# Joining the two words of a double with an integer addition on the weights' conversion

## The chip, the cores and the metric

One core of a Trainium2 chip runs the kernel. The metric is the device time of one execution in microseconds (us). The core has a matrix engine (TensorE, PE in the rows; PEld is its weight load), VectorE (DVE), ScalarE (ACT), GpSimd (POOL) and SyncE (SP), which issues the DMA transfers here. Each engine works through its own instructions in the order in which they stand and waits where an operand isn't ready.

## The reference

An attention with 32 inducing points is followed by two feed-forward layers. With x of 12480 x 128, inducing of 32 x 128 and four weight matrices of 262144 elements each:

```
def mab(q, kv):
    s = scale * (q @ kv.transpose(0, 2, 1)); s = s - s.max(-1, keepdims=True)
    a = np.exp(s); a /= a.sum(-1, keepdims=True) + 1e-09
    return a @ kv
h = mab(I, x)                      # 32 x 128
x = mab(x, h)                      # 12480 x 128
h = x @ w_in;   x = np.maximum(0.01 * h, h) @ w_out            # 2048 wide
h = x @ w2_in;  g = where(h >= 1, h, where(h <= -1, 0, (h + 1) ** 2 / 4));  x = g @ w2_out
```

The weights arrive as doubles (the drawn values are multiplied to float64), that is, as two 32-bit words per element, low word first.

## The kernel before

**Stages.** First the x tokens are read in nine bands and the inducing points attend to them (lines 330 to 378); that gives HT. Then 25 chunks of some 500 tokens each pass through the rest. The loop from line 604 runs over column steps k: chunk c and block j of 128 hidden columns, k = 16 c + j. In one step PE makes block j of the hidden layer of chunk c (line 626, from Gs, which is HT times the first weights, and the attention weights aT). ACT rounds it to hi (line 629). DVE makes the rest lo (line 636), or at j = 4, 8, 12 of chunk 0 and 3, 9, 14 of the next chunks ACT makes r and POOL subtracts (lines 633, 634). D1 = 4 steps later PE multiplies hi and lo with the second weights, whi[0] and wlo[0], in three matmuls (L577 in all rows of PE, since a helper records them). The second layer (weights n = 2, 3) starts 86 steps later and runs beside the first until the end.

**Weights.** The four matrices are cut into 16 units (n, q), n the matrix and q a quarter of 512 columns. A unit's words come by one DMA of 512 KB into a tile wraw (10 buffers, column 2i the low word and 2i + 1 the high word of element i). The generator convert(n, q) turns them into fp32 for n = 0 (tile w1) and into a rounded part whi and a rest wlo for n = 1 to 3. Its buffers cva and cvb exist three times. Two units run at a time; each call of work(1) takes one of them, in turns, to its next yield. Line 339 to 347, 586 to 600 and 710 to 713 call it: in the bands as WORK_S says, four times around the first attention of a chunk, once in each of the steps k = 0 to 15 and once in three steps after that. So the place of a conversion's instruction in an engine's order follows from how many yields lie ahead of it. The order of the units is (0,0), (1,0), (0,1), (0,2), (1,1), (0,3), (1,2), (1,3), then n = 2 and n = 3.

**One unit before.** ACT takes the high word times 2^-112 without its sign (L108), DVE the sign bit (L109), DVE joins them by shift and or (L111): cva is the high word's value as fp32. DVE cuts out its power of two (L113) and multiplies the low word by 2^-52 and by this power (L118): cvb is the low word's value. For n = 0 DVE adds both (L121). For n > 0 ACT rounds cva to whi (L116), and POOL takes cva minus whi (L125) plus cvb (L126) for wlo; for (1,0) and (1,1) PE does that instead with three matmuls by unit matrices (L134, L135, L136) and ACT reads the result (L137).

**What waits for it.** hidden(q, .) multiplies HT with a quarter of w1 into Gs (PE L403, ACT L407, DVE L410); linear(.) folds the slope of the first layer into Qs (L425 to L445), and the loop reads whi and wlo of a matrix from the step on where ensure() stands.

Of the kernel before, what the change touches and what calls it, by code (L numbers as in the profile page):

```python
# [9 lines left out]
F32 = mybir.dt.float32  # L10
F32R = mybir.dt.float32r
I32 = mybir.dt.int32
U32 = mybir.dt.uint32
AF = mybir.ActivationFunctionType
ALU = mybir.AluOpType
# [18 lines left out]
QW = 512  # L34
# [31 lines left out]
PE_LO = 2  # L66
# [6 lines left out]
def moe_kernel(ctx: ExitStack, tc, x_d, xf_d, xl_d, xt_d, it_d, w1_d, w2_d, w3_d, w4_d, y_d):  # L73


    nc = tc.nc
# [7 lines left out]
    cv = fill.enter_context(tc.tile_pool(name="cv", bufs=3, side="right"))  # L84
    xp = fill.enter_context(tc.tile_pool(name="xp", bufs=1, side="right"))
    ps = ctx.enter_context(tc.tile_pool(name="ps", bufs=1, space=PSUM))
    bank = [ps.tile([128, 512], F32, name=f"bank{i}", tag=f"bank{i}") for i in range(8)]
# [10 lines left out]
    def convert(n, q):  # L98

        t = raws.pop((n, q))
        up, low = t[:, :, 1], t[:, :, 0]
        sl = slice(q * QW, (q + 1) * QW)
        a = cv.tile([128, QW], F32, name="cva")
        b = cv.tile([128, QW], F32, name="cvb")
        au, bu = a.bitcast(U32), b.bitcast(U32)
        nc.scalar.activation(a, up.bitcast(F32), AF.Abs, scale=WORD_SCALE)  # L108
        nc.vector.tensor_scalar(out=bu, in0=up.bitcast(U32), scalar1=0x80000000, scalar2=None, op0=ALU.bitwise_and)  # L109
        yield  # L110
        nc.vector.scalar_tensor_tensor(out=au, in0=au, scalar=3, in1=bu, op0=ALU.logical_shift_left, op1=ALU.bitwise_or)  # L111
        yield
        nc.vector.tensor_scalar(out=bu, in0=au, scalar1=0xFF800000, scalar2=None, op0=ALU.bitwise_and)  # L113
        if n:
            hi, lo = whi[n - 1][:, sl], wlo[n - 1][:, sl]
            nc.scalar.activation(hi, a, AF.Copy)  # L116
        yield
        nc.vector.scalar_tensor_tensor(out=b, in0=low.bitcast(U32), scalar=2.0 ** -52, in1=b, op0=ALU.mult, op1=ALU.mult)  # L118
        if n == 0:
            yield  # L120
            nc.vector.tensor_tensor(out=w1[:, sl], in0=a, in1=b, op=ALU.add)  # L121
        elif n == 1 and q < PE_LO:
            lows.append((bank[2 + q], a, b, hi, lo))
        else:
            nc.gpsimd.tensor_tensor(out=a, in0=a, in1=hi.bitcast(F32), op=ALU.subtract)  # L125
            nc.gpsimd.tensor_tensor(out=lo, in0=a, in1=b, op=ALU.add)  # L126

    lows = []

    def low_parts(n):  # L130

        for _ in range(n):
            s, a, b, hi, lo = lows.pop(0)
            nc.tensor.matmul(s, lhsT=ident, rhs=a, start=True, stop=False)  # L134
            nc.tensor.matmul(s, lhsT=ident, rhs=b, start=False, stop=False)  # L135
            nc.tensor.matmul(s, lhsT=nidentr, rhs=hi, start=False, stop=True)  # L136
            nc.scalar.activation(lo, s, AF.Copy)  # L137

# [8 lines left out]
    def work(n, until=len(units)):  # L147

        for _ in range(n):
            while len(running) < 2 and to_convert and len(units) - len(to_convert) < until:  # L150
                running.append((to_convert[0], convert(*to_convert.pop(0))))
            if not running:
                return
            u, r = running.pop(0)
            if next(r, "end") != "end":
                running.append((u, r))
            else:
                done.add(u)
                if ahead:
                    load_next_w()  # L160

    def ensure(n, j):

        while (n, j * 128 // QW) not in done:
            work(1)
        if n == 1:
            low_parts(len(lows))
# [17 lines left out]
    w1 = fillp.tile([128, FF], F32, name="w1")  # L185
    whi, wlo = [wts.tile([128, FF], F32R, name="whi0", tag="whi0")], [wts.tile([128, FF], F32R, name="wlo0", tag="wlo0")]
# [32 lines left out]
    ident = const.tile([128, 128], F32, name="ident")  # L219
# [110 lines left out]
    for s in range(NS_B):  # L330
        ready = len(lows)
        scores(s)
        if s:
            turn(s - 1)
        warm(WARM_A.get(s, 0))
        if s + 1 < NS_B and s + 1 not in xT:
            by_channel(s + 1)
        exps(s)
        work(WORK_S[s][0], UNTIL_S[s])
        if s:  # L340
            gather(s - 1)
            add_up(s - 1)
        if s >= NS_B - XL:
            warm(WARM_B)
        if s == NS_B - 3:
            low_parts(ready)
        work(WORK_S[s][1], UNTIL_S[s])
# [29 lines left out]
                            in1=rden[:, None, :].to_broadcast([C, 3, M]), op=ALU.mult)  # L377
# [226 lines left out]
    for k in range(NS + LAG * NJ + OB + D2):  # L604
# [18 lines left out]
        if in_a:  # L623
# [3 lines left out]
            hi = hp1.tile([128, CW], F32R, name="hi1")[:, :w]  # L627
            lo = hp1.tile([128, CW], F32R, name="lo1")[:, :w]
            nc.scalar.activation(hi, p1, AF.Relu)  # L629
            h1[k] = hi, lo  # L630
            if j in (POOL_LO1 if kb >= 0 else POOL_LO1_FILL if c else POOL_LO1_0):
                r = r1p.tile([128, CW], F32, name="r1")[:, :w]
                nc.scalar.activation(r, p1, AF.Relu)  # L633
                nc.gpsimd.tensor_tensor(out=lo, in0=r, in1=hi.bitcast(F32), op=ALU.subtract)  # L634
            else:
                nc.vector.scalar_tensor_tensor(out=lo, in0=p1, scalar=0.0, in1=hi.bitcast(F32),  # L636
                                               op0=ALU.max, op1=ALU.subtract)
# [6 lines left out]
        if kb - 2 in gs:  # L644
            g = gs.pop(kb - 2)
            hi = hp3.tile([128, CW], F32R, name="hi3")[:, :g.shape[1]]
            lo = hp3.tile([128, CW], F32R, name="lo3")[:, :g.shape[1]]
# [15 lines left out]
        if kb - 1 in sqs:  # L663
# [4 lines left out]
                                           op0=ALU.max, op1=ALU.add)  # L668
            gs[kb - 1] = g
        if late:  # L670
            lo, g, hi = late
            nc.vector.tensor_tensor(out=lo, in0=g, in1=hi.bitcast(F32), op=ALU.subtract)
        if 0 <= kh < NS:
# [5 lines left out]
            if jh == NJ - 1:  # L679
                mm(px, Qs, aT.pop(ch), False, True)  # L680
                hi = x2p.tile([128, CW], F32R, name="x2hi")[:, :w]
                lo = x2p.tile([128, CW], F32R, name="x2lo")[:, :w]
# [18 lines left out]
        if k in HIDDEN:  # L701
            q = 1 + HIDDEN.index(k)
# [3 lines left out]
        if k == HIDDEN[-1]:  # L706
            low_parts(len(lows))
# [58 lines left out]
```

## Time and profile before

| | us |
|---|---|
| median of 3 runs | 1000.36 (999.27 to 1000.88) |
| the profiled execution | 1000.86 |
| its span in the trace | 998.9 |
| PE busy in the span | 980.3 |
| DVE busy | 812.6 |
| ACT busy | 798.7 |
| POOL busy | 642.9 |

The span runs from the first to the last instruction that the profiler recorded; some 2 us of the execution lie outside. The granted clock of TensorE was 0.999 of full speed over the span. Rows name instructions by the line of the kernel, the operation and the tiles (out<-in); a wait stands in brackets as the idle time ahead of an instruction and what released it.

### The profile page before, as it was taken

What the parts mean: (1) busy time and instruction counts of PE and PEld (TensorE: products, weight loads), DVE (VectorE), ACT (ScalarE), POOL (GpSimd) and SP (SyncE); (2) the same over time, 40 slices, a digit from 0 to 9 for tenths busy, and PEclk for the clock granted to TensorE, in tenths of its full rate; (3) what the DMA queues carried; (4) which work ended last, traced back from release to release, by engine and by line L of the source; (5) the groups of instructions that cost most, each with busy time, mean ns of one, the idle gap of its engine ahead of it and who ended that gap; (6) DMA issues with size and microseconds to landing.
All of it is one profiled execution on the core that took longest, in us unless ns stands there. A gap on an engine that the chain in (4) does not pass through costs nothing.

```text
span 998.9 us, 14767 instructions
## 1 busy us (share of the span) xinstructions
PE 980.3 (98%) x4632; PEld 797.0 (80%) x4632; DVE 812.6 (81%) x1358; ACT 798.7 (80%) x1464; POOL 642.9 (64%) x513
## 2 busy tenths in 40 slices
PE   8889999999999999999999999999999999999998
PEld 6656777888878888878888878888888888888886
DVE  4799888877779877779877779777788777789997
ACT  4576778888878888878888878888878888889997
POOL 0044546667766666666766666666667667778886
PEclk9999999999999999999999999999999999999999
DMA  9801011100002000001000001000000000000000
GB/s 351 322 28 38 1 58 43 42 1 11 11 1 68 27 1 12 11 27 52 17 1 12 11 22 41 11 1 11 12 1 27 11 1 12 11 12 11 12 10 22
DMA packets 18863, 34.22 MB, mean 34 GB/s; under 512 B 10928, under 2 KB 14128, under 8 KB 17504
## 3 DMA queue, kind: packets, MB, share of 16 engines
q1 hardware_dynamic: 18784, 33.28, 9.6%
q8 instruction: 36, 0.59, 0.2%
q14 instruction: 43, 0.35, 0.1%
HBM read 22.66 MB, written 6.39 MB: 29 GB/s over the span
## 4 chain that ended last, share of the span: by engine, by line
PE 92%; DVE 5%; ACT 1%; issue 1%; POOL 1%; ACTq 0%; POOLq 0%; DVEq 0%
PE bank L577 87%; DVE lo L636 2%; PE bank L263 1%; PE bank L275 1%; PE bank L308 1%; DVE cva L111 1%; PE bank L474 1%; PE bank L233 0%; PE bank L326 0%; ACT hi L629 0%; PE bank L297 0%; POOL lo L634 0%; DVE cvb L113 0%; POOL wlo L126 0%; DVE cvb L118 0%
## 5 line engine op out<-in xcount | busy, mean ns | idle before, releaser
L653 POOL TENSOR_TENSOR lo<-g,hi 128x500 fp32r<-128x500 f32 (+2 forms) x392 | 496.5, 1270 | 205.8 <-PE bank L577 150.1
L629 ACT ACTIVATE hi<-bank 128x500 fp32r<-128x500 f32 (+2 forms) x400 | 233.9, 588 | 133.2 <-PE bank L577 128.8
L577 PE MATMUL bank<-lo,whi 128*128 128x500 f32 (+2 forms) x800 | 311.5, 389 | 3.2 <-POOL lo L634 2.8
L577 PE MATMUL bank<-hi,whi 128*128 128x500 f32 (+2 forms) x800 | 311.1, 389 | 0.0
L577 PE MATMUL bank<-hi,wlo 128*128 128x500 f32 (+2 forms) x800 | 310.4, 388 | 0.0
L661 DVE TENSOR_SCALAR cl<-bank 128x500 f32<-128x500 f32 (+2 forms) x400 | 268.0, 670 | 43.6 <-PE bank L577 37.5
L641 ACT ACTIVATE sq<-cl,half 128x500 f32<-128x500 f32 (+2 forms) x400 | 284.3, 711 | 17.7 <-DVE cl L661 11.9
L667 DVE SCALAR_TENSOR_TENSOR g<-bank,sq 128x500 f32<-128x500 f32 (+2 forms) x400 | 267.8, 669 | 34.9 <-ACT sq L641 34.6
L636 DVE SCALAR_TENSOR_TENSOR lo<-bank,hi 128x500 fp32r<-128x500 f32 (+2 forms) x305 | 203.9, 672 | 73.7 <-ACT hi L629 72.7
L648 ACT ACTIVATE hi<-g 128x500 fp32r<-128x500 f32 (+2 forms) x400 | 245.7, 614 | 0.8 <-DVE g L667 0.5
L577 PEld LDWEIGHTS bank<-lo,whi 128*128 128x128 f32 x800 | 150.2, 188 | 37.4 <-POOL lo L634 4.5
L577 PEld LDWEIGHTS bank<-hi,wlo 128*128 128x128 f32 x800 | 150.4, 188 | 30.3
L577 PEld LDWEIGHTS bank<-hi,whi 128*128 128x128 f32 x800 | 150.5, 188 | 30.2 <-ACT y L694 0.4
L634 POOL TENSOR_TENSOR lo<-r,hi 128x500 fp32r<-128x500 f32 (+2 forms) x95 | 121.9, 1284 | 69.7 <-ACT r L633 61.2
L577 PE MATMUL bank<-x2hi,whi 128*128 128x500 f32 (+2 forms) x400 | 156.4, 391 | 0.0
L577 PE MATMUL bank<-x2hi,wlo 128*128 128x500 f32 (+2 forms) x400 | 155.1, 388 | 0.0
L577 PE MATMUL bank<-x2lo,whi 128*128 128x500 f32 (+2 forms) x400 | 155.0, 388 | 0.0
L577 PE MATMUL bank<-aTg,Gs 96*128 96x500 f32 x352 | 138.2, 393 | 0.2 <-DVE lo L636 0.2
L577 PEld LDWEIGHTS bank<-x2hi,whi 128*128 128x128 f32 x400 | 75.9, 190 | 16.9 <-DVE g L667 1.4
L577 PEld LDWEIGHTS bank<-x2hi,wlo 128*128 128x128 f32 x400 | 75.9, 190 | 15.0
L577 PEld LDWEIGHTS bank<-x2lo,whi 128*128 128x128 f32 x400 | 75.2, 188 | 15.4
L577 PEld LDWEIGHTS bank<-aTg,Gs 96*128 96x128 f32 x352 | 66.1, 188 | 17.6 <-DVE g L667 2.9
(134 smaller groups left out, 476.4 us busy)
## 6 DMA issues: line engine op xcount, KB each, us to landing
wraw<-in_w SPq DMA_DIRECT2D x16, 512.0 KB, 9.7
out_y<-y SPq DMA_DIRECT2D x22, 250.0 KB, 2.0
xb<-in_x SPq DMA_DIRECT2D x5, 1024.0 KB, 14.2
xtm<-in_xt SPq DMA_DIRECT2D x4, 1024.0 KB, 4.8
aTg<-hT SPq DMA_DIRECT2D x32, 62.5 KB, 2.0
xl<-in_xl SPq DMA_DIRECT2D x1, 1024.0 KB, 15.6
xts<-in_xt SPq DMA_DIRECT2D x2, 512.0 KB, 5.8
aTg<-lT SPq DMA_DIRECT2D x16, 62.5 KB, 2.0
```

The costliest lines, as they stand in the source:

```text
L111: nc.vector.scalar_tensor_tensor(out=au, in0=au, scalar=3, in1=bu, op0=ALU.logical_shift_left, op1=ALU.bitwise_or)
L263: nc.tensor.transpose(ps_t[:, i * p:(i + 1) * p], xb[s][:, q, b, :], ident[:p, :p])
L275: nc.tensor.matmul(p[q * M:(q + 1) * M, :w], lhsT=iT, rhs=xT[s][:, q * w:(q + 1) * w], start=True, stop=True)
L577: nc.tensor.matmul(out, lhsT=w, rhs=x, start=start, stop=stop)
L629: nc.scalar.activation(hi, p1, AF.Relu)
L634: nc.gpsimd.tensor_tensor(out=lo, in0=r, in1=hi.bitcast(F32), op=ALU.subtract)
L636: nc.vector.scalar_tensor_tensor(out=lo, in0=p1, scalar=0.0, in1=hi.bitcast(F32), op0=ALU.max, op1=ALU.subtract)
L641: nc.scalar.activation(sq, cl, AF.Square, scale=-0.5, bias=half)
L648: nc.scalar.activation(hi, g, AF.Copy)
L653: nc.gpsimd.tensor_tensor(out=lo, in0=g, in1=hi.bitcast(F32), op=ALU.subtract)
L661: nc.vector.tensor_scalar(out=cl, in0=p3, scalar1=1.0, scalar2=-1.0, op0=ALU.min, op1=ALU.max)
L667: nc.vector.scalar_tensor_tensor(out=g, in0=b3[(kb - 1) % 3][:, :w], scalar=-1.0, in1=sq, op0=ALU.max, op1=ALU.add)
```

## The change

The low word is no longer scaled to a float of its own. ACT multiplies it by 2^-29 into an integer of 0 to 8, in place in the raw tile (new line 110); that is its value in last places of the fp32 number that the high word gives. DVE joins sign and magnitude as before, but into cvb, and an integer addition adds the two words: on DVE for n = 0 and n = 1 (new lines 116 and 120), on POOL for n = 2 and 3 (new line 122). DVE's L113 and L118 go, and DVE's float addition of n = 0 becomes the integer one. whi is now the rounded sum, so that POOL only subtracts (new line 128), and PE has one matmul less for (1,0) and (1,1). A unit of n = 0 takes three calls of work instead of five. From line 106 on the new line numbers are the old ones plus 1.

```diff
@@ -103,36 +103,37 @@
         up, low = t[:, :, 1], t[:, :, 0]
         sl = slice(q * QW, (q + 1) * QW)
         a = cv.tile([128, QW], F32, name="cva")
-        b = cv.tile([128, QW], F32, name="cvb")
-        au, bu = a.bitcast(U32), b.bitcast(U32)
+        b = cv.tile([128, QW], I32, name="cvb")
+        r = low
+        au, bu, ai = a.bitcast(U32), b.bitcast(U32), a.bitcast(I32)
         nc.scalar.activation(a, up.bitcast(F32), AF.Abs, scale=WORD_SCALE)
+        nc.scalar.activation(r, low.bitcast(U32), AF.Copy, scale=2.0 ** -29)
         nc.vector.tensor_scalar(out=bu, in0=up.bitcast(U32), scalar1=0x80000000, scalar2=None, op0=ALU.bitwise_and)
         yield
-        nc.vector.scalar_tensor_tensor(out=au, in0=au, scalar=3, in1=bu, op0=ALU.logical_shift_left, op1=ALU.bitwise_or)
+        nc.vector.scalar_tensor_tensor(out=bu, in0=au, scalar=3, in1=bu, op0=ALU.logical_shift_left, op1=ALU.bitwise_or)
         yield
-        nc.vector.tensor_scalar(out=bu, in0=au, scalar1=0xFF800000, scalar2=None, op0=ALU.bitwise_and)
-        if n:
-            hi, lo = whi[n - 1][:, sl], wlo[n - 1][:, sl]
-            nc.scalar.activation(hi, a, AF.Copy)
+        if n == 0:
+            nc.vector.tensor_tensor(out=w1[:, sl].bitcast(I32), in0=b, in1=r, op=ALU.add)
+            return
+        hi, lo = whi[n - 1][:, sl], wlo[n - 1][:, sl]
+        if n == 1:
+            nc.vector.tensor_tensor(out=ai, in0=b, in1=r, op=ALU.add)
+        else:
+            nc.gpsimd.tensor_tensor(out=ai, in0=b, in1=r, op=ALU.add)
+        nc.scalar.activation(hi, a, AF.Copy)
         yield
-        nc.vector.scalar_tensor_tensor(out=b, in0=low.bitcast(U32), scalar=2.0 ** -52, in1=b, op0=ALU.mult, op1=ALU.mult)
-        if n == 0:
-            yield
-            nc.vector.tensor_tensor(out=w1[:, sl], in0=a, in1=b, op=ALU.add)
-        elif n == 1 and q < PE_LO:
-            lows.append((bank[2 + q], a, b, hi, lo))
-        else:
-            nc.gpsimd.tensor_tensor(out=a, in0=a, in1=hi.bitcast(F32), op=ALU.subtract)
-            nc.gpsimd.tensor_tensor(out=lo, in0=a, in1=b, op=ALU.add)
+        if n == 1 and q < PE_LO:
+            lows.append((bank[2 + q], a, hi, lo))
+        else:
+            nc.gpsimd.tensor_tensor(out=lo, in0=a, in1=hi.bitcast(F32), op=ALU.subtract)
 
     lows = []
 
     def low_parts(n):
 
         for _ in range(n):
-            s, a, b, hi, lo = lows.pop(0)
+            s, a, hi, lo = lows.pop(0)
             nc.tensor.matmul(s, lhsT=ident, rhs=a, start=True, stop=False)
-            nc.tensor.matmul(s, lhsT=ident, rhs=b, start=False, stop=False)
             nc.tensor.matmul(s, lhsT=nidentr, rhs=hi, start=False, stop=True)
             nc.scalar.activation(lo, s, AF.Copy)
```

How the instructions stand is shown at three places. ACT, at the first aT of chunk 0 (the matmul that starts the loop over column steps reads it), before:

```order
L551 ACTIVATE ea<-ea 122x128
L562 ACTIVATE s<-ea 122x4x32
L563 ACTIVATE s<-ea 122x4x32
L407 ACTIVATE Gs<-bank_83 96x512
L108 ACTIVATE cva<-wraw 128x512
L573 ACTIVATE aT_735<-bank_81 96x488
L116 ACTIVATE whi_92<-cva 128x512
L629 ACTIVATE hi_741<-bank_84 128x488
```

and after the change:

```order
L552 ACTIVATE ea<-ea 122x128
L563 ACTIVATE s<-ea 122x4x32
L564 ACTIVATE s<-ea 122x4x32
L408 ACTIVATE Gs<-bank_83 96x512
L123 ACTIVATE whi_92<-cva 128x512
L574 ACTIVATE aT_735<-bank_81 96x488
L123 ACTIVATE whi_92<-cva 128x512
L630 ACTIVATE hi_741<-bank_84 128x488
```

One rounding to whi, that of unit (1,2), has come to stand ahead of aT, where only the first operation of a unit stood. DVE, at the end of the last band (mrow is the minimum over the bands, from which the rest of the first attention follows), before:

```order
L109 TENSOR_SCALAR cvb<-wraw 128x512
L312 SCALAR_TENSOR_TENSOR D<-D,alpha,ssum 128x1
L322 SCALAR_TENSOR_TENSOR R<-R,alpha,bank_88 128x128
L111 SCALAR_TENSOR_TENSOR cva<-cva,cvb 128x512
L113 TENSOR_SCALAR cvb<-cva 128x512
L356 TENSOR_REDUCE mrow<-bank_81 1x32
L357 COPY mrow<-mrow 1x96
```

and after the change:

```order
L111 TENSOR_SCALAR cvb<-wraw 128x512
L313 SCALAR_TENSOR_TENSOR D<-D,alpha,ssum 128x1
L323 SCALAR_TENSOR_TENSOR R<-R,alpha,bank_88 128x128
L113 SCALAR_TENSOR_TENSOR cvb<-cva,cvb 128x512
L116 ISA w_91<-wraw,cvb 128x1024
L357 TENSOR_REDUCE mrow<-bank_81 1x32
L358 COPY mrow<-mrow 1x96
```

Where the power of two was cut out, the integer addition stands; it is written as an instruction on 1024 halves of words instead of 512 words. POOL, from the rests lo of chunk 0 on that ACT and POOL make (lo and the matrices n = 2 share the queue), before:

```order
L634 TENSOR_TENSOR lo_787<-r_789,hi_786 128x488
L634 TENSOR_TENSOR lo_855<-r_857,hi_854 128x488
L125 TENSOR_TENSOR cva<-cva,whi_663 128x512
L126 TENSOR_TENSOR wlo_664<-cva,cvb 128x512
```

and after the change:

```order
L635 TENSOR_TENSOR lo_786<-r_788,hi_785 128x488
L122 TENSOR_TENSOR cva<-cvb,wraw 128x512 x2
L128 TENSOR_TENSOR wlo_663<-cva,whi_662 128x512
L635 TENSOR_TENSOR lo_852<-r_854,hi_851 128x488
L128 TENSOR_TENSOR wlo_663<-cva,whi_662 128x512
```

The additions of the first two units of n = 2 stand right behind the first lo, and the subtraction of the second behind the next lo. Over the whole program DVE has 1327 rows instead of 1359, POOL 510 instead of 518, ACT 1473 instead of 1457 and PE 4164 instead of 4166.

## Rows read from the trace of the kernel before

**Rows 1.** The chain that ended last, its shares of the span by engine.

```profile
PE 92%; DVE 5%; ACT 1%; issue 1%; POOL 1%; ACTq 0%; POOLq 0%; DVEq 0%
```

**Rows 2.** Busy us by stage: bands, start of the loop, second stage, the rest.

```profile
core 0: us, PE busy (x) PEld busy (x) DVE busy (x) ACT busy (x) POOL busy (x), PEclk, DMA share, GB/s
13.00:53.00 40.00, 34.87 (x408) 24.23 (x403) 31.25 (x84) 24.71 (x60) 0.00 (x0) 1.00 0.87 344
53.00:84.00 31.00, 27.72 (x150) 19.28 (x151) 30.02 (x51) 21.92 (x47) 16.45 (x12) 1.00 0.06 18
84.00:153.00 69.00, 65.52 (x293) 51.93 (x292) 58.32 (x102) 51.48 (x101) 32.20 (x24) 1.00 0.10 27
153.00:998.00 845.00, 841.72 (x3726) 692.84 (x3724) 690.72 (x1113) 696.94 (x1248) 593.56 (x471) 1.00 0.05 17
```

**Rows 3.** The chain in order of time: start, us, engine, tile, line.

```profile
34.90 0.86 PE bank L135 x2
...
37.67 0.61 ACT eT L299
...
43.16 0.70 DVE cva L111
43.88 0.43 DVE cvb L113
44.31 0.20 DVE mrow L356
...
52.49 0.47 ACT aT L573
53.01 0.49 PE bank L577
...
83.36 0.29 DVE Qs L445
```

**Rows 4.** PE's waits from 84 to 153, from timelines: idle before and releaser.

```profile
96.16 0.49 PE L577 MATMUL bank<-lo,whi 128*128 128x496 f32 x1 [0.19 <-DVE lo L636]
...
100.44 0.49 PE L577 MATMUL bank<-lo,whi 128*128 128x496 f32 x1 [0.38 <-POOL lo L634]
...
131.52 0.49 PE L577 MATMUL bank<-lo,whi 128*128 128x500 f32 x1 [0.41 <-POOL lo L634]
...
134.10 0.49 PE L577 MATMUL bank<-lo,whi 128*128 128x500 f32 x1 [0.26 <-DVE lo L636]
...
138.49 0.49 PE L577 MATMUL bank<-lo,whi 128*128 128x500 f32 x1 [1.39 <-POOL lo L634]
```

**Rows 5.** POOL's timeline ahead of the last of these waits.

```profile
135.95 1.29 POOL L126 TENSOR_TENSOR wlo<-cva,cvb 128x512 fp32r<-128x512 f32 x1 [3.05 <-DVE cvb L118]
137.21 1.23 POOL L634 TENSOR_TENSOR lo<-r,hi 128x500 fp32r<-128x500 f32 x1
```

**Rows 6.** Groups of instructions from 53 to 84: count, busy us, mean ns, idle before.

```profile
L111 DVE SCALAR_TENSOR_TENSOR cva<-cva,cvb 128x512 uint32<-128x512 uint32 x6 | 4.9, 818 | 0.0
L109 DVE TENSOR_SCALAR cvb<-wraw 128x512 uint32<-128x512 uint32 x5 | 3.9, 787 | 0.0
L118 DVE SCALAR_TENSOR_TENSOR cvb<-wraw,cvb 128x512 f32<-128x512 uint32 x5 | 3.4, 689 | 0.1
L113 DVE TENSOR_SCALAR cvb<-cva 128x512 uint32<-128x512 uint32 x5 | 2.5, 510 | 0.0
...
L108 ACT ACTIVATE cva<-wraw 128x512 f32<-128x512 f32 x4 | 2.7, 673 | 0.0
...
L125 POOL TENSOR_TENSOR cva<-cva,whi 128x512 f32<-128x512 f32 x5 | 6.7, 1347 | 54.6 <-DVE cvb L113 54.0 <-PE bank L577 0.6
L634 POOL TENSOR_TENSOR lo<-r,hi 128x488 fp32r<-128x488 f32 x3 | 4.1, 1355 | 2.2 <-ACT r L633 2.2
```

**Rows 7.** Timeline of ACT from 129.5 to 140: start, us, instruction (four at once here).

```profile
130.01 2.03 ACT L629 ACTIVATE hi<-bank 128x500 fp32r<-128x500 f32 x4
```

**Rows 8.** Timeline of DVE, just before the loop starts.

```profile
51.97 0.68 DVE L410 SCALAR_TENSOR_TENSOR Gs<-bank,Gs 32x512 fp32r<-32x512 f32 x1 [0.39 <-DMA wraw<-in_w]
```

## The prediction

> **What bounds the kernel now.** The first view is the chain that ended last: PE holds 92% of it, DVE 5% [rows 1]. The busy time by stage says where the other engines count [rows 2]. From 153 us to the end PE is busy for 841.7 of 845 us; nothing that the conversion does reaches there, since the units are done by then. Between 53 and 84 us DVE is busy for 30.0 of 31 us, PE for 27.7 and ACT for 21.9: DVE is the bound of this stage. In the 40 us before 53, the bands, no engine is full (PE 34.9), and there the chain in order of time shows what is late [rows 3]: at 37.7 ACT's eT, at 43 two conversion instructions of DVE ahead of mrow, at 52.5 aT, which releases the loop's first matmul at 53.0; at 83.4 it is DVE again, with Qs, which closes chunk 0. From 84 to 153 PE is the bound and stops now and then; five of these stops are for a lo that came late [rows 4], together 0.19 + 0.38 + 0.41 + 0.26 + 1.39 = 2.6 us. The longest shows how: POOL stood 3.05 us before L126, waiting for DVE's L118, and the lo that PE needed was queued behind it [rows 5].
>
> So 100 us of 1000 can move, and there DVE's load, ACT's order and POOL's queue are to be read apart.
>
> **The change part by part.** Units need 28 DVE instructions less, 16 ACT instructions more, and two fp32 matmul pairs of PE and two POOL operations less.
>
> Prices. L113 is 0.51 us and L118 0.69 us between 53 and 84 [rows 6]. The new ACT operation reads and writes as many words as L108, 0.67 us; ACT's instructions overlap a little (four of 0.58 take 2.03 us, that is 0.48 each [rows 7]), so I charge 0.67 - 0.11 = 0.56 us; its bounds are 0.48 and 0.67. No row has an integer addition. On DVE it has two inputs from SBUF, as L118 has: not under 0.69; and it is issued on 1024 halves of words, which at most doubles L118: 1.38. I take 0.85, nearer the low end, since the bytes are those of 512 words. [...] No row before shows an operation on halves. On POOL the nearest rows are the float operations L125 and L634, 1.35 us each [rows 6]: I take 1.35; the upper bound is twice that, 2.7, if the integer way goes through the data twice.
>
> Bands, to 53 us. PE loses one L135 pair, 0.86 us at 34.9 [rows 3], but whi of that unit now waits for DVE's addition, and eT stands behind it on ACT: some +0.4 at 37.7 instead of a gain. Ahead of mrow stood L111 and L113 (0.70 + 0.43); now L113 and L116 of the new numbers (0.70 + 0.85): +0.4. Together +0.75.
>
> Start of the loop. ACT now has one more whi ahead of aT, as the order shows. That whi waits for DVE: L410 ends at 51.97 + 0.68 = 52.65 [rows 8], the joining takes 0.70, the addition 0.85: 54.2; whi itself occupies ACT for 0.56: aT could begin at 54.75, and with the 0.75 above at 55.5. Before it began at 52.4 to 52.5. The first matmul of the loop follows it by about 0.6: 56.1 instead of 53.0, +3.1 us (the 0.75 is in it).
>
> The stage from 53 to 84, now from 56.1. DVE: 30.0 - 2.5 - 3.4 (all L113 and L118), minus one L111 and one L109 that are done before it because units of n = 0 take fewer calls (0.8 + 0.8), plus two additions of n = 1 (1.7): 24.2 us. ACT: 21.9 plus four new operations at 0.56: 24.2 us, and ACT now also waits. For n = 2 whi needs POOL's addition, and POOL has the lo of the first layer ahead of it: after ACT's r come 1.35 + 1.35 us of POOL, of which ACT fills about 1.1 with its next two instructions: a wait of 1.6. The second addition ends 1.35 later, and ACT has 0.95 of its own in between: 0.4. This occurs for two pairs of units, at k = 5, 6 and 13, 14 (the second time with a little less on ACT in between, 1.8): 1.6 + 0.4 + 1.8 + 0.4 = 4.2 us. Then DVE's last steps to Qs, 0.4 more than inside ACT's time. Sum: 56.1 + 24.2 + 4.2 + 0.4 = 84.9, where Qs released PE at 83.7 (83.36 + 0.29 [rows 3] and the step over): +1.2. So ACT takes DVE's place as the bound, and of the 3.1 us 1.9 come back. The second L135 pair is in this stage and hidden, since PE is not the bound.
>
> The stage from 84 to 153. L118 isn't there to hold POOL, and DVE has 1.2 us less for each unit: the five waits of 2.6 us [rows 4] go, and with each about 0.15 of restart: -3.4. Against it stand waits of POOL's addition in the same queue; I put one of 0.5 in. Net -2.9.
>
> After 153 nothing: 0.
>
> Sum: +1.2 - 2.9 = -1.7 us against the profiled execution's own 1000.86. The median of the runs is 1000.36, 0.5 below it; the forecast for a median is 1000.36 - 1.7 = 998.7 us. 0.2% or 2 us is about what a measurement can tell from no change, so this lies just within it.
>
> **The rivals.**
>
> *B, the lag of ACT is absorbed.* PE needs hi and lo only four steps after they are made (D1 = 4), so hi may be late by as much. If ACT's 4.2 us of waits and half of the start's delay are taken up by that, Qs comes at about 83.5 to 84 with DVE's 24.2 us ahead of it: then -1.4 there instead of +1.2, with -2.9 behind it: -4.3, 996.1 us. For it speaks that DVE was the full engine and ACT had 9 us free; against it that ACT's order is fixed and aT stands at its head.
>
> *C, the addition on POOL is slow (the other side).* Four additions lie on ACT's path between 56 and 85. Each us that one takes beyond 1.35 delays hi by as much four times, and in the second stage lo behind it. It decides from -1.7 + 4 x = +2, x = 0.9, that is from 2.3 us each. At 2.7: 4 x 1.35 = +5.4, and -1.7 + 5.4 = +3.7: 1004.1 us. For it: no integer operation of POOL is in the trace, and one input is a column of pairs. Against it: POOL's float operations with two inputs lie between 1.2 and 1.4 us [rows 5, 6]. [...]
>
> *D, the change does less than it says.* If DVE's addition goes through 1024 halves one by one, at 1.38 us it costs more than the L113 or L118 that it replaces in n = 0 and n = 1. The path has it three times (ahead of eT, mrow and aT), 0.53 us more each, of which the first is in part covered: about +1.3, and the sum is -0.4: 1000.0 us.
>
> **How the numbers follow.** The forecast has 0.45, B 0.27, C 0.14, D 0.14. Faster by over 0.2%: B's 0.27 and the better part of the forecast's spread (0.10): 0.37. Slower by over 0.2%: C and 0.02 from the forecast and D: 0.16. Within: 0.47. The forecast's own range is 997 to 1000.5 (0.16 us either way for each of some ten DVE additions and ACT operations, and the 4.2 us of waits that may be half or one and a half of that). The range that is to hold 8 in 10 takes in B with its bound, 995.8, and above D and the milder half of C: 1002.2.
>
> **What would show it.** The new ACT line 110 at 0.67 us and DVE's addition between 0.69 and 1.38; the first L578 matmul (L577 before) behind aT at 56 instead of 53; between there and 85 DVE idle by some 5 us and ACT's whi with idle time that POOL's cva ended; Qs at about 85; behind it the waits for lo gone; from 153 on the distances as before. The prediction is wrong if aT isn't delayed (then B or better), if POOL's addition exceeds 2.3 us (C), or if the waits after 84 us stay though L118 is gone: then the stage gives nothing back, and the sum is +1.2 + 0.5, 1002.1 us.

## The result: 6 us slower

The changed kernel took 1005.98 us (median of 10 runs, 1003.23 to 1009.66), the kernel before 999.85 (10 runs, 997.70 to 1000.92); the ratio is 1.0061, with a 95% interval of 1.0043 to 1.0080. The forecast was 998.7, the range 995.8 to 1002.2. The mean granted clock of the ten runs of the changed kernel was 0.988, 0.993 or 0.995, and the runs with the lowest clock are the longest (1003.2 to 1003.8 us at 0.995, 1008.1 to 1009.7 at 0.988); the runs of before that were taken beside the experiments stand at 0.997 to 0.999.

The profiled execution took 1003.28 us, span 1001.5, at 0.995: it is one of the four short ones, and no trace shows what the longer ones add. Counted in single instructions, as the page does, DVE has 1330 instead of 1358, POOL 511 instead of 513, ACT 1480 instead of 1464 and PE 4628 instead of 4632; that is the change as the prediction counts it. The row counts in the section on the change take neighbours of one kind as one row and so show another difference. First the chain by engine in the page of the changed kernel, which answers to [rows 1]:

```profile
PE 94%; DVE 2%; ACT 2%; issue 1%; POOL 1%; DMA 0%; POOLq 0%; ACTq 0%; DVEq 0%
```

DVE has less of the path, as forecast (5% to 2%), and PE has more of it, though it has less work. The busy time by stage says why; the column to read is the third from the right, the granted clock. The rows answer to [rows 2]:

```profile
core 0: us, PE busy (x) PEld busy (x) DVE busy (x) ACT busy (x) POOL busy (x), PEclk, DMA share, GB/s
53.00:84.00 31.00, 28.97 (x147) 19.87 (x147) 21.09 (x36) 23.52 (x51) 16.99 (x13) 0.91 0.06 18
84.00:153.00 69.00, 65.50 (x283) 51.48 (x284) 49.34 (x91) 50.81 (x102) 25.82 (x20) 0.98 0.10 27
```

The same view in steps of 2 us:

```profile
48.00:50.00 2.00, 0.55 (x5) 0.41 (x4) 1.17 (x5) 0.99 (x3) 0.00 (x0) 1.00 0.25 94
50.00:52.00 2.00, 0.00 (x0) 0.00 (x0) 1.97 (x4) 0.25 (x1) 0.00 (x0) 0.99 0.00 0
52.00:54.00 2.00, 1.11 (x2) 0.72 (x3) 0.26 (x1) 1.66 (x4) 1.54 (x2) 0.50 0.00 0
54.00:56.00 2.00, 2.00 (x4) 0.90 (x3) 0.67 (x1) 0.87 (x3) 0.96 (x1) 0.50 0.03 8
56.00:58.00 2.00, 2.00 (x4) 0.90 (x3) 1.35 (x2) 0.94 (x3) 0.00 (x0) 0.50 0.00 0
58.00:60.00 2.00, 2.00 (x5) 0.74 (x4) 1.38 (x3) 2.00 (x5) 0.00 (x0) 0.80 0.00 0
...
84.00:86.00 2.00, 0.00 (x0) 0.00 (x0) 1.93 (x3) 0.06 (x1) 1.23 (x1) 1.00 0.00 0
86.00:88.00 2.00, 1.99 (x5) 1.66 (x6) 0.62 (x1) 1.24 (x3) 0.00 (x0) 0.53 0.00 0
88.00:90.00 2.00, 2.00 (x9) 1.62 (x8) 1.82 (x6) 1.23 (x4) 0.00 (x0) 0.62 0.00 0
```

TensorE's granted clock is 0.50 of full speed from 52.0 to 58.7 us and again from 86.2 to 89.4, each time after a stretch in which PE did nothing. Before, the clock was 1.00 in all these stages [rows 2]. The ends of the two empty stretches stand in the timeline of PE, of the changed kernel:

```profile
52.89 0.78 PE L578 MATMUL bank<-aT,Gs 96*128 96x488 f32 x1 [2.96 <-ACT aT L574]
...
86.02 0.71 PE L578 MATMUL bank<-aT,Qs 96*128 96x488 f32 x1 [2.39 <-DVE Qs L446]
```

and of the kernel before:

```profile
53.01 0.49 PE L577 MATMUL bank<-aT,Gs 96*128 96x488 f32 x1 [0.76 <-ACT aT L573]
...
83.70 0.49 PE L577 MATMUL bank<-aT,Qs 96*128 96x488 f32 x1 [1.04 <-DVE Qs L445]
```

What made aT late is in the chain of the changed kernel:

```profile
49.65 0.68 DVE Gs L411
...
50.36 0.69 DVE cvb L113
51.05 0.61 DVE cva L120
...
51.75 0.63 ACT whi L123
52.38 0.47 ACT aT L574
...
52.89 0.78 PE bank L578
53.67 1.71 PE bank L404 x2
```

This is the sequence that the order showed: Gs, joining, addition, whi, aT. And it ends with the price: an L404 pair takes 1.71 us, twice the 0.86 of the same pair (L403) in the chain of the kernel before.

The two spans can't be compared from zero. PE's 20 matmuls for warming up took 4.53 us in the profiled execution before and 3.76 in this one, and by the third band from the end this execution is 3.1 us ahead. (The granted clock doesn't explain it: its rows stand at 1.00 there in both.) This lead differs from execution to execution of either kernel: the matmul that was at 32.76 us in the kernel before is at 31.33 in the kernel before with a gap, and at 29.66 to 33.00 in those with the integer addition. So the times below count from the matmul L308 (L309 after the change) that was at 32.76 in the kernel before and at 29.66 after it, behind the same wait for eT of 0.7 us. Columns: to the loop's first matmul, from there to the matmul with Qs, from there to the end of the span.

| kernel | to first matmul | to Qs | to the end | sum |
|---|---|---|---|---|
| before | 20.25 | 30.69 | 915.20 | 966.14 |
| changed | 23.23 | 33.13 | 915.48 | 971.84 |
| aT first | 22.33 | 32.12 | 914.17 | 968.62 |
| PE warm, one gap | 26.04 | 30.66 | 915.44 | 972.14 |
| PE warm, four gaps | 23.28 | 30.65 | 914.24 | 968.17 |
| before with a gap | 23.86 | 32.14 | 914.97 | 970.97 |
| additions on DVE | 25.94 | 35.26 | 916.96 | 978.16 |
| whi early for n = 1 | 19.93 | 32.28 | 914.08 | 966.29 |
| whi early for n = 2, 3 | 25.81 | 28.95 | 912.69 | 967.45 |
| whi early | 19.95 | 28.20 | 912.71 | 960.86 |
| whi early, aT first | 19.88 | 27.68 | 912.52 | 960.08 |
| whi early, additions on DVE | 19.98 | 28.72 | 911.60 | 960.30 |

Each row is one profiled execution, so differences under 1 us aren't read from it. The changed kernel loses 5.7 us by it: 3.0 to the loop, 2.4 up to Qs, 0.3 behind. The whole profiled executions differ by 2.4 us, since this one had the lead at the start, and the medians by 6.1. In four of these executions (aT first, PE warm in one gap, additions on DVE, whi early for n = 2, 3) the clock fell in the bands too, which it didn't in the changed kernel's; that is in their first column.

### The profile page after: what moved, and what is told of

It is laid out like the page before. It is cut to its first block, busy times and chain, and to the rows that moved or that the text cites. A ratio compares the mean times of both kernels' runs of the same rounds, so it can differ in the third digit from the quotient of the medians.

```text
span 1001.5 us, 14739 instructions
## 1 busy us (share of the span) xinstructions
PE 979.9 (98%) x4628; PEld 796.2 (80%) x4628; DVE 795.1 (79%) x1330; ACT 806.3 (81%) x1480; POOL 638.9 (64%) x511
## 4 chain that ended last, share of the span: by engine, by line
PE 94%; DVE 2%; ACT 2%; issue 1%; POOL 1%; DMA 0%; POOLq 0%; ACTq 0%; DVEq 0%
PE bank L578 89%; PE bank L264 1%; DVE cvb L113 1%; ACT hi L630 1%; PE bank L276 1%; DVE lo L637 1%; PE bank L475 1%; PE bank L309 0%; PE bank L404 0%; PE bank L327 0%; PE bank L234 0%; POOL cva L122 0%; ACT cva L109 0%; PE bank L298 0%; DMA xt<-in_xt 0%
```

## The experiments

The theory: whi now waits for the addition, ACT with it, and PE empties; the wait costs itself and the clock behind it. The rivals: the waits alone; the additions on POOL; the order at the loop's start.

**aT first.** One swap on ACT, by one step of work moved behind aT; the other engines keep their order.

```diff
-WORK_T = (2, 1, 2, 2)
+WORK_T = (2, 1, 1, 3)
```

> The changed kernel with one swap on ScalarE: aT ahead of the rounding to whi that stood before it; all other engines keep their order. Theory (TensorE's idle time of 2.96 us before the loop's first matmul makes its clock fall to half for some 7 us): the idle time falls to about 0.8 us, the clock stays at full speed there, and the kernel is 4 to 5 us faster than the changed one, about 1001 to 1002 us. Rival (the loop's start is late and nothing else): at most the 2.2 us of delay come back, 1003.5 to 1004 us, with the clock as it was.

1002.19 us (12 runs, 998.70 to 1009.33), ratio to before 1.0038 (1.0020 to 1.0056). The gap ahead of the first matmul went to 0.66 us, but the clock fell in the bands already:

```profile
46.00:48.00 2.00, 2.00 (x15) 2.00 (x14) 1.58 (x6) 1.56 (x3) 0.00 (x0) 0.70 0.91 291
48.00:50.00 2.00, 2.00 (x8) 1.56 (x8) 0.60 (x4) 0.00 (x0) 0.00 (x0) 0.50 0.63 254
```

PE had waited 2.06 us for eT and 1.13 for mrow ahead of that (0.75 and 0.76 before). Behind the 2.41 us ahead of Qs it didn't fall in this execution. So the same gap is followed by a fall in one execution and not in another. The runs spread over 10 us, and their clock with them (0.997 in the run of 998.70 us, 0.983 in that of 1009.33). The median lies just above what the theory said, but the clock didn't stay up as it said, so this run doesn't tell the delay from the clock.

**PE warm in one gap.** 22 more warm-up matmuls behind the last PE work ahead of the loop.

```diff
     attend(0, 5)
+    warm(22)
     work(WORK_T[2])
```

> The changed kernel with 22 more warm-up matmuls in TensorE's idle time before the loop's first matmul; nothing else is moved, and that first matmul still waits for the late aT. Theory (the clock): the clock stays at full speed from 52 to 60 us, the first matmul begins at the same time after the bands as in the changed kernel, and 2 to 4 us come back: 1002 to 1004 us. Rival (the delay alone): no change, 1005.5 to 1006.5 us.

1004.64 us (5 runs, 1004.41 to 1006.74), ratio 1.0067 (1.0052 to 1.0081), between what the theory and the rival said. Inconclusive: in the profiled execution the clock had fallen from 37 to 41 and from 46 to 53 us, behind the waits in the bands, and the loop started 2.8 us later than in the changed kernel. The stage to Qs then ran at full clock and took 30.66 instead of 33.13 us.

**PE warm in four gaps.** The same, with 14 matmuls ahead of the late eT, 5 ahead of mrow and 16 ahead of Qs.

```diff
+        if s == 7:
+            warm(14)
         if s:
             gather(s - 1)
...
-WARM_T = (3, 4, 4, 5, 6)
+WARM_T = (8, 4, 4, 5, 6)
...
+                if ch == 0:
+                    warm(16)
                 mm(px, Qs, aT.pop(ch), False, True)
```

> The changed kernel with warm-up matmuls in TensorE's four long waits (14 ahead of the eT that came 2.1 us late, 5 ahead of mrow, 22 ahead of the loop's first matmul, 16 ahead of Qs); the conversion is untouched. Theory (the clock's falls cost 4 to 6 of the 6 us lost, the waits themselves the rest): the granted clock stays at 0.999 as before and the time is 1000 to 1002.5 us. Rival (the waits alone cost it): 1005 to 1006.5 us though the clock is at 0.999.

1000.51 us (12 runs, 999.78 to 1002.88), ratio 1.0015 (1.0006 to 1.0024); the clock of the runs was 0.998 to 1.000. The row of the granted clock is 1.00 from 0 to 100 us, and aT comes as late as in the changed kernel:

```profile
49.98 2.84 PE L327 MATMUL bank<-twice,identr 128*128 128x256 f32 x22
53.11 0.49 PE L580 MATMUL bank<-aT,Gs 96*128 96x488 f32 x1 [0.29 <-ACT aT L576]
```

From the third band to the loop it takes 23.28 us as there (23.23), but the stage to Qs 2.5 us less. By the ratios the clock costs 1.0061 - 1.0015 = 0.46%, 4.6 of the 6.1 us; the ends of the two intervals leave 2 to 7. The conversion is untouched here, so it is shown that most of the loss goes when PE is kept at work; which of the four gaps costs what isn't. The rest, 0.15% or 1.5 us, is left of the waits after what the change gives back.

**Before with a gap.** The other direction: the kernel before, with 11 copies on ACT ahead of aT.

```diff
     work(WORK_T[2])
+    for _ in range(11):
+        nc.scalar.activation(denb, ones, AF.Copy)
     attend(0, 6)
```

> The kernel before, with 11 copies of 128x128 on ScalarE ahead of aT (2.2 us), so that TensorE idles about 3 us there, as in the changed kernel, without any of its conversion. Theory (the clock): it falls to half for some 7 us behind the gap and the kernel is 3 to 6 us slower than before, 1003 to 1006 us. Rival (the lag takes the delay up, and the conversion's order costs the time in the changed kernel): 0 to 2.2 us, 1000 to 1002 us.

1004.30 us (5 runs, 1003.23 to 1004.74), ratio 1.0055 (1.0043 to 1.0067). PE idled 4.36 us, which is 3.60 more than before (0.76) where 2.2 more were meant, and the clock fell without any of the new conversion:

```profile
52.00:54.00 2.00, 0.00 (x0) 0.00 (x0) 1.22 (x3) 1.83 (x6) 0.00 (x0) 0.67 0.03 8
54.00:56.00 2.00, 0.81 (x2) 0.69 (x3) 0.00 (x0) 1.60 (x5) 0.26 (x1) 0.50 0.00 0
56.00:58.00 2.00, 2.00 (x4) 0.79 (x4) 0.67 (x1) 0.87 (x2) 1.00 (x1) 0.50 0.00 0
58.00:60.00 2.00, 2.00 (x5) 0.82 (x4) 1.61 (x3) 1.01 (x3) 0.12 (x1) 0.62 0.00 0
```

The loop starts 3.6 us later and Qs comes 5.1 later. The clock's fall is in the difference, so this run alone doesn't price the delay; but nothing of the delay came back by the time of Qs.

**whi early.** whi is rounded from cvb, the high word's value, ahead of the addition; the rest is still the sum minus whi. The kernel before rounds it from the high word too.

```diff
         hi, lo = whi[n - 1][:, sl], wlo[n - 1][:, sl]
+        nc.scalar.activation(hi, b.bitcast(F32), AF.Copy)
         if n == 1:
...
-        nc.scalar.activation(hi, a, AF.Copy)
```

> The changed kernel with whi rounded from the high word's value, before the integer addition, so that ScalarE waits for no addition; the rest lo is still the sum minus whi. If ScalarE's waits for GpSimd's additions are what makes Qs late in the stage to 85 us: 3 us come back there, Qs's idle time on TensorE falls under 1.5 us and the second fall of the clock (86 to 89 us) is gone, 1001 to 1003 us; the first fall stays, since whi still stands ahead of aT. If those waits are covered by the lag of four steps: under 1 us, 1005 to 1006 us.

992.47 us (6 runs, 991.89 to 995.04), ratio to before 0.9945 (0.9931 to 0.9959): by the medians 13.5 us under the changed kernel, far more than I expected, and 6.7 under the kernel before (11.6 and 5.5 by the ratios). All three places gain: PE's wait for aT and for eT (2.07 to 0.98), the stage to Qs, and the one behind it:

```profile
49.69 0.48 PE L578 MATMUL bank<-aT,Gs 96*128 96x488 f32 x1 [0.72 <-ACT aT L574]
...
77.89 0.49 PE L578 MATMUL bank<-aT,Qs 96*128 96x488 f32 x1
```

Qs isn't waited for any more. I had expected the first fall of the clock to stay, since whi still stands ahead of aT; the gap went instead (2.96 us to 0.72), for it is the wait for the addition, not the place of whi, that made it. The clock is not at full speed throughout here either: it fell from 59 to 62 us, with PE at work; the waits marked in the 10 us ahead of it were 0.72 and 0.65 us.

```profile
60.00:62.00 2.00, 2.00 (x6) 1.22 (x4) 1.82 (x5) 1.52 (x4) 2.00 (x2) 0.50 0.00 0
```

**whi early for one part.** The same for n = 1 alone and for n = 2, 3 alone. The edit for n = 1 is shown; the other has the two conditions exchanged.

```diff
+        if n == 1:
+            nc.scalar.activation(hi, b.bitcast(F32), AF.Copy)
...
-        nc.scalar.activation(hi, a, AF.Copy)
+        if n > 1:
+            nc.scalar.activation(hi, a, AF.Copy)
```

> The changed kernel with whi from the high word for n = 1 alone; for n = 2 and 3 it still waits for GpSimd's addition. Theory (each wait of ScalarE costs its own delay and a fall of the clock behind it): the idle time before the loop's first matmul falls from 2.96 to 0.7 us and the clock doesn't fall there, the one before Qs stays at 2.4 us with its fall behind it: 6 to 8 us of the 13.5 between the changed kernel and whi from the high word throughout, 998 to 1000 us. Rival (only the additions on GpSimd matter, the start is taken up later): 1004 to 1006 us.

> The changed kernel with whi from the high word for n = 2 and 3 alone; for n = 1 it still waits for VectorE's addition. Theory: the idle time before the loop's first matmul stays near 3 us with the clock's fall behind it, the one before Qs goes and so does its fall: the other 5 to 7 us of the 13.5, 999 to 1001 us. If only the additions on GpSimd matter: 992 to 994 us.

n = 1 alone: 1000.17 us (11 runs, 996.31 to 1002.89), ratio 1.0011 (0.9998 to 1.0023). n = 2, 3 alone: 1000.01 us (11 runs, 997.91 to 1000.92), ratio 1.0003 (0.9993 to 1.0012). Each takes back about 6 of the 13.5 us (5.0 and 5.8 of the 11.6 by the ratios), in the place that the theory names: the first column of the table for n = 1, the other two for n = 2, 3, where the first column is longer by the fall of the clock in the bands. What the theory said of the clock failed for n = 1: it fell at the loop's start behind a wait of only 0.72 us, and not behind the 2.41 us ahead of Qs.

```profile
50.44 0.77 PE L581 MATMUL bank<-aT,Gs 96*128 96x488 f32 x1 [0.72 <-ACT aT L577]
```

```profile
50.00:52.00 2.00, 1.56 (x4) 0.86 (x4) 1.97 (x4) 1.48 (x3) 0.40 (x1) 0.60 0.03 8
52.00:54.00 2.00, 2.00 (x6) 0.85 (x4) 1.14 (x3) 1.04 (x2) 2.00 (x2) 0.54 0.00 0
```

PE had waited 1.38 us for s just ahead of that, as in the kernel before. So the waits cost what the table says, but a fall of the clock can't be put down to one wait.

**The additions on DVE.** All integer additions on DVE, where they are shorter; whi waits for them.

```diff
-        if n == 1:
-            nc.vector.tensor_tensor(out=ai, in0=b, in1=r, op=ALU.add)
-        else:
-            nc.gpsimd.tensor_tensor(out=ai, in0=b, in1=r, op=ALU.add)
+        nc.vector.tensor_tensor(out=ai, in0=b, in1=r, op=ALU.add)
```

> The changed kernel with the integer addition of n = 2 and 3 on VectorE too; whi still waits for it. Each such addition takes 0.65 us there instead of 1.5 on GpSimd and doesn't stand behind lo in GpSimd's queue. If ScalarE's waits for GpSimd's additions (2.0 + 0.2 + 2.3 + 0.2 us from 56 to 85) are what makes Qs late: they fall under 1 us together, Qs's idle time goes, and the kernel is 4 to 8 us faster than the changed one, 998 to 1002 us. If it is enough that whi waits for any addition: within 2 us of the changed one, 1004 to 1007 us. The gap before the loop's first matmul stays in both.

1010.50 us (4 runs, 1009.97 to 1013.50), ratio 1.0120 (1.0103 to 1.0137): slower still, which neither expectation had. The groups of whi on ACT up to Qs, first of the changed kernel and then of this one (idle before in the last column):

```profile
L123 ACT ACTIVATE whi<-cva 128x512 fp32r<-128x512 f32 x5 | 3.1, 630 | 4.7 <-POOL cva L122 4.7
```

```profile
L120 ACT ACTIVATE whi<-cva 128x512 fp32r<-128x512 f32 x5 | 3.1, 629 | 7.8 <-DVE cva L119 7.8
```

The timeline of DVE shows why:

```profile
68.53 0.68 DVE L119 CUSTOM_DVE_ANT_0 cva<-wraw,cvb 128x1024 uint16<-128x1024 uint16 x1
70.43 0.67 DVE L634 SCALAR_TENSOR_TENSOR lo<-bank,hi 128x488 fp32r<-128x488 f32 x1 [1.22 <-ACT hi L627]
...
71.53 0.68 DVE L119 CUSTOM_DVE_ANT_0 cva<-wraw,cvb 128x1024 uint16<-128x1024 uint16 x1
```

The shorter addition (0.68 us, against 1.48 in the mean on POOL) makes the longer wait here (7.8 us against 4.7), since in DVE's order the second addition of a pair stands behind a lo, that lo waits for ACT's hi, and hi stands behind the whi that waits for the first addition. On POOL the two additions follow each other at once: in the changed kernel a pair takes 3.03 us from 64.92.

**whi early with two further changes.** With aT first as well, and with the additions on DVE as well.

> The kernel with whi from the high word, and aT ahead of the whi that stood before it. If the order at the loop's start still costs there (aT waits for VectorE's joining through that whi, some 1 us): 991 to 992 us, 1 us under whi from the high word alone (992.5). If not: 992 to 993 us.

> whi from the high word, and all integer additions on VectorE. GpSimd loses eight additions of 1.5 us, VectorE gains eight of 0.65. If GpSimd's additions still hold lo back in its queue: 1 to 2 us under whi from the high word alone, 990.5 to 991.5 us. If VectorE is the engine that is full there: 993 to 995 us.

aT first: 992.56 us (5 runs, 991.68 to 994.22), ratio 0.9937 (0.9924 to 0.9951), the same as without it. Additions on DVE: 995.63 us (6 runs, 992.01 to 996.71), ratio 0.9960 (0.9944 to 0.9976), 3 us more by the medians. In the table's terms its profiled execution (995.09 us) sums to 960.30 us, like whi early alone; it reached the matmul from which the table counts at 33.00 us instead of 29.74, and up to there both run the same instructions. So in this execution the 3 us lie ahead of anything that the edit touches; the other runs have no trace.

## Why the prediction was wrong

**The start of the loop** was forecast 3.1 us late; it was 3.0. The joining took 0.69 (0.70 forecast) and DVE's addition 0.68 to 0.75 (0.85 taken; the lower bound was 0.69). PE's wait for eT grew by 1.3 us, from which the lost matmuls took 0.9, and the wait for mrow by 0.4: some 0.4 each, as said. The mechanism was right.

**The step that failed** is the one after it: "the stage from 53 to 84, now from 56.1" was summed from ACT's work and waits, as if PE ran at its speed of before. The rows that I had showed a granted clock of 1.00 in every stage, and waits of PE of at most 1.4 us around the loop's start and Qs; I never asked what a wait of 3 us does to the clock. In the profiled execution the granted clock stood at 0.50 instead of 1.00 for 6.8 us, from 52.0 us on, that is from within that wait, and again for 3.4 us behind the wait for Qs. The experiment with PE warm in four gaps prices this at 4.6 us. A fall of the clock behind the forecast gap of 3 us was the rival that I left out: 4.6 us more than -1.7 are +2.9. The other 3.2 us up to the +6.1 measured are two terms that were mis-sized, in the next two paragraphs: at full clock (PE warm in four gaps) Qs came 3.0 us later than before, not 1.2, and the stage behind it gave back 1.0, not 2.9.

**ACT's waits** were forecast at 1.6 + 0.4 + 1.8 + 0.4 = 4.2 us in this stage; they were 2.0 + 0.2 + 2.3 + 0.2 = 4.7. But the stage at full clock takes 30.65 us (PE warm in four gaps), not 28.8. The term that was too small is the last one, "DVE's last steps to Qs, 0.4": ACT's part of Qs ended at 83.12, DVE's at 85.97, because two lo, L484 and L488 stood ahead of it on DVE; with PE warm the tail was as long (ACT 80.84, DVE 83.70). L488 took 1.22 us with POOL at work, and 0.41 before. The changed kernel's rows of DVE, then the row of the same operation (L487) before:

```profile
84.42 1.22 DVE L488 TENSOR_TENSOR eg<-eg,mg 128x256 f32<-128x256 f32 x1
85.68 0.28 DVE L446 TENSOR_TENSOR Qs<-bank,Qs 32x128 fp32r<-32x128 f32 x1
```

```profile
82.93 0.41 DVE L487 TENSOR_TENSOR eg<-eg,mg 128x256 f32<-128x256 f32 x1
```

Late hi make late lo (DVE waited 1.75 us for a hi at 80.2 us and 0.61 at 81.4), and these are in DVE's queue when Qs is due. So ACT's bound isn't followed by a short tail but by DVE's backlog.

**The stage from 84 to 153** was forecast 2.9 us shorter, since nothing holds POOL any more. At full clock everything behind Qs was 1.0 shorter (914.24 against 915.20), with whi early 2.5. In the 70 us behind Qs PE is idle for 3.5 us in the kernel before and for 2.1 with PE warm in four gaps:

```profile
83.70:153.70 70.00, 66.52 (x296) 52.81 (x297) 59.03 (x103) 51.73 (x101) 32.20 (x24) 1.00 0.09 27
```

```profile
83.76:153.76 70.00, 67.93 (x300) 53.32 (x301) 50.33 (x93) 53.06 (x105) 25.82 (x20) 1.00 0.09 27
```

Of the 2.6 us of waits for a lo that are marked, 0.4 are left. So the gain is there, but whi waits for POOL in this stage too (9.2 us up to 160 us, 4.7 of them before Qs), and PE now waits for hi (0.42 and 0.20 us where it is marked): that takes more than the 0.5 that I put in. The 0.15 of restart for each wait, -0.75 in the sum, was an estimate that no row and no run shows; a matmul behind a wait shows 0.49 us, and 0.39 without one.

**The prices** otherwise held: ACT's new operation 0.68 us; POOL's addition 1.48 in the mean (1.30 to 1.76) against 1.35 taken, under the 2.3 from which rival C decides. Rival D fell: 1024 halves took 0.69 us, as long as L118 with 512 words [rows 6], and not the 1.38 that D put in. Rival B (the lag takes ACT's delay up) fell with PE warm in four gaps: at full clock the loop starts 3.0 us late, and Qs is 3.0 us late still. What B promised, 996.1 us, needs ACT's waits removed, not absorbed; that is whi early, at 992.5.

## What to carry to other kernels

A sum of busy times is only as good as the clock that stands behind it: here waits of 2.96 and 2.39 us instead of 0.76 and 1.04 went with 6.8 and 3.4 us at a granted clock of 0.50. So where an edit makes TensorE wait longer, price the work behind the wait at half clock as well, and try the edit once with filler matmuls in the gap to see the share of the clock (4.6 of the 6.1 us here). And look at what stands behind an operation that gains an operand from another engine's queue: whi waited 2.13 us for DVE's addition with aT right behind it, and 4.7 us in all for POOL's additions up to Qs, with hi behind it. Here the change was worth 5.5 to 6.7 us, but only once ScalarE's rounding took its operand from before the addition.

## What the runs showed of the hardware that I had not expected

TensorE's clock fell behind gaps of 2.06 (eT, additions on DVE), 2.39 and 2.96 (Qs and aT, the changed kernel) and 4.36 us (aT, before with a gap), and not in every execution: behind 2.41 us ahead of Qs it stayed at 1.00 with aT first and with whi early for n = 1, and behind 2.07 ahead of eT in the changed kernel. It also fell where the waits ahead were 1.38 and 0.72 us (whi early for n = 1), and with whi early behind waits of 0.72 and 0.65 us. The integer addition on 1024 halves of words took 0.69 us on DVE, as long as L118, a float operation on 512 words (0.69 [rows 6]), although one input is a column of pairs. L113, which reads two tiles in SBUF, took 0.69 us in the middle of its 16 times and 1.73 when it ran beside POOL's lo (the same operation of the kernel before, L111, 0.69 and up to 1.49); L488 above shows the like, 0.41 and 1.22. That POOL is the cause wasn't tested. One L113 and the lo beside it:

```profile
63.77 1.73 DVE L113 SCALAR_TENSOR_TENSOR cvb<-cva,cvb 128x512 uint32<-128x512 uint32 x1
```

```profile
63.56 1.40 POOL L635 TENSOR_TENSOR lo<-r,hi 128x488 fp32r<-128x488 f32 x1 [8.60 <-ACT r L634]
```
